# Another step order in a copy out of PSUM, pooled queries by two additions, and a new instruction order

## The chip, the core and the metric

The kernel runs on one core of one Trainium2 chip. TensorE (PE) multiplies matrices into PSUM, VectorE (DVE) and ScalarE (ACT) work element by element and read PSUM, GpSimd (POOL) works in SBUF and issues DMAs, SyncE (SP) issues DMAs only. The metric is the device time of the whole program in microseconds, given as the median of several runs.

## What is computed

Two layers follow each other. The first is an "hourglass" attention over 8 batches of 8 heads, 576 positions of 64 values each; the second sends each of the 4608 resulting rows to one of 8 experts. Cut to what matters:

```python
q_d = q.reshape(B, H, Sd, 4, D).mean(axis=3)      # the same for k_d, v_d
out_d = sm_attn(q_d, k_d, v_d)                    # softmax attention over 144 means
out_up = np.repeat(out_d, 4, axis=2)
mask = np.abs(pos[:, None] - pos[None, :]) < 4    # a band of 7 positions
out_local = softmax(where(mask, scale * q @ k.T, -1e9)) @ v
x = (out_up + out_local) as rows of 512
logits = x @ w_gate; e_idx = argmax(logits)       # one expert for each row
out[row] = gate_w * sigmoid(x @ w_output_gate)[e] * (relu(x @ w1[e]) @ w2[e])
```

## The kernel before, in words

The attention is done in 32 units, one for each pair of heads of a batch (`u = 4 b + hp`). After the four units of a batch comes its `gate` part, which routes the rows and stores them in DRAM. The experts run last, in tiles of 128 rows: `unit` gathers rows, transposes them, multiplies by w1 (L1074), takes the relu (L1016 on ACT, L1018 on DVE), multiplies by w2 (L1090), scales (L1099) and scatters (L1021).

A unit of attention begins with `prep(u)`. PE transposes q and then k of two heads (L641) from `blk` into a PSUM tile, which holds 576 f16 columns on 128 partitions. In PSUM the column of position 8 n + c is 72 c + n: positions that follow each other lie 72 columns apart. For q, DVE copies the tile as it is into `qT` (L651), and the reduce of L656 sums four positions each into `qd`, reading in steps of 72 columns. For k, ACT copies the tile into `kT` in the order of the positions (L665): it reads PSUM column after column, and writes SBUF in steps of 8 elements, 16 bytes. Then DVE sums four neighbours of `kT` into `kd` (L670) and scales them (L672).

`scores(u)` needs all of these. PE multiplies `kd` with `qd` (L690) and pools v (L695), ACT copies the pooled v (`vd`, L701), PE writes the other scores (L709, L717, L725), and ACT takes their exponential (`e`, L730). `values(u)` has the four groups of f32 matmuls L749, L755, L761 and L773. ACT forms the reciprocal of the sums as a logarithm and an exponential (`r`, L780 and L782), DVE multiplies (`u` L786, `xl` L794), POOL adds both parts into `xT` (L799), and ACT casts the result (L803). Two buffers hold `qT`, `qd`, `kT`, `kd`, `e` and `r`. Five PSUM tiles (S0, S1 of one bank, P0 to P2 of two) serve every user in turn.

Each engine carries out its instructions in the order in which they were written. That order comes from `Plan`: each task has an engine, an assumed duration, dependences and a priority; the plan takes, over and over, the task that can start first by its assumed times. `ADJ` adds a number to the priority of each kind of task. The assumed duration of L665 is 0.65 us before and after the change.

Of the kernel before, what the change touches and what calls it, by code (L numbers as in the profile page):

```python
# [8 lines left out]
F32 = mybir.dt.float32  # L9
F16 = mybir.dt.float16  # L10
I32 = mybir.dt.int32
ALU = mybir.AluOpType
AX = mybir.AxisListType
# [7 lines left out]
HB = 72  # L21
# [23 lines left out]


ADJ = {
# [6 lines left out]
    "mek": -365.54, "mek0": -101.99, "meq": 70.66, "meq0": 312.43, "out": -166.06, "prepk": -56.67,  # L54
# [5 lines left out]
}  # L60


# [3 lines left out]
def _ap(t, ap_list, extra_off=0):  # L66
    return bass.AP(tensor=t.tensor, offset=t.offset + extra_off, ap=ap_list)
# [263 lines left out]
def kernel(  # L331
# [11 lines left out]
    nc = tc.nc  # L343
    B, H, S, D = q.shape
# [15 lines left out]
    sb = ctx.enter_context(tc.tile_pool(name="sb", bufs=2))  # L360
# [12 lines left out]
    def v_qk(t):  # L373
        return t[0:HB].rearrange("p (h c) -> p h c", h=HP)
# [34 lines left out]
    plan = Plan()  # L409
    qb, vb = {}, {}  # L410

    def prio(u, kind, more=0.0):
        return 10.0 * u + OFF[kind] + more
# [79 lines left out]
    C = {}  # L493
# [121 lines left out]
        C["late"] = ts  # L615


    st = {}
    xb = {}

    def t16(T):
        return T.tile.bitcast(F16)[:, 0:S]

    def own(u):
        return "0" if u < 3 else ""

    def prep(u):
        b, hp = u // NP, u % NP
        d = st[u] = {}
        half = hp // 2  # L630
        h0 = 2 * (hp % 2)
        loads = [t for h in (2 * hp, 2 * hp + 1) for t in qb[b, half, "t"][h]]
        for i, nm in enumerate("qk"):
            T = Buf(r_T)
            src = qb[b, half][i]

            def fn(T=T, src=src):
                o = t16(T)
                for c in range(8):
                    for h in range(2):  # L640
                        nc.tensor.transpose(o[64 * h:64 * h + 64, HB * c:HB * c + HB],  # L641
                                            v_qk(src.tile)[:, h0 + h, D * c:D * c + D], id16[0:HB, 0:HB])
            hold = [Buf(r_qT), Buf(r_qd)] if i == 0 else [Buf(r_kT), Buf(r_kd)]
            tp = plan.add("PE", 0.29, fn, deps=[loads[0 + i], loads[2 + i], C["id"]], uses=[T, src] + hold,
                          prio=prio(u, "prep", i * 0.5), mode=12864, lat=0.1, name="prep" + nm + own(u), slow=0.5,
                          stream=(0.24, 0.45), ins=32)
            mean = hold[1]
            if i == 0:
                qT = d["qT"] = hold[0]
                d["qd"] = mean  # L650
                ev = plan.add("DVE", 0.46, lambda T=T, qT=qT: nc.vector.tensor_copy(qT.tile, t16(T)),  # L651
                              deps=[tp], uses=[T, qT], prio=prio(u, "ev"), name="qT" + own(u))

                def fn(mean=mean, qT=qT):
                    s = qT.tile[:, 0:1]
                    nc.vector.tensor_reduce(mean.tile.rearrange("p (n j i) -> p n j i", j=2, i=6),  # L656
                                            _ap(s, [s.ap[0], [6, 12], [4 * HB, 2], [1, 6], [HB, 4]]), axis=AX.X, op=ALU.add)
                e2 = plan.add("DVE", 0.75, fn, deps=[ev], uses=[qT, mean], prio=prio(u, "e2"), name="meq" + own(u))
            else:
                kT = d["kT"] = hold[0]  # L660
                d["kd"] = mean

                def fn(T=T, kT=kT):
                    s = t16(T)[:, 0:1]
                    nc.scalar.copy(kT.tile[:, 4:4 + S].rearrange("p (n c) -> p c n", c=8),  # L665
                                   _ap(s, [s.ap[0], [HB, 8], [1, HB]]))
                ev = plan.add("ACT", 0.65, fn, deps=[tp, C["z"]], uses=[T, kT], prio=prio(u, "ev", 0.5), name="kT" + own(u))

                def fn(mean=mean, kT=kT):
                    nc.vector.tensor_reduce(mean.tile.rearrange("p (g n) -> p g n", n=32)[:, :, 0:SW // 2],  # L670
                                            kT.tile[:, 4:4 + S].rearrange("p (g n m) -> p g n m", g=NGB, m=4), axis=AX.X, op=ALU.add)
                    nc.vector.tensor_scalar(mean.tile, mean.tile, scalar1=1.0 / 16, scalar2=None, op0=ALU.mult)  # L672
                e2 = plan.add("DVE", 0.93, fn, deps=[ev, C["z"]], uses=[kT, mean], prio=prio(u, "e2", 0.5), name="mek" + own(u))
            d[f"ev{i}"], d[f"e2{i}"] = ev, e2

    def scores(u):
# [427 lines left out]
    with tc.manual_schedule():  # L1104
# [8 lines left out]
        for u in range(NU):  # L1113
            prep(u)
# [16 lines left out]
        n = 0  # L1131
# [33 lines left out]
    with tc.If(v_most > 0):  # L1165
# [9 lines left out]
        for e in range(E):  # L1175
# [6 lines left out]
            with tc.For_i(0, n_more, 1):  # L1182
# [3 lines left out]
                for j in range(NJ * B):  # L1186
# [6 lines left out]
                    out=xg[:, 0, :], out_offset=None, in_=xs_dram.ap(),  # L1193
                    in_offset=bass.IndirectOffsetOnAxis(ap=fari, axis=0), bounds_check=N, oob_is_err=False)
                xgT, hs, yt = r_xgT.make(), r_hs.make(), r_y.make()
                t16 = singles[0].bitcast(F16).rearrange("p (j c n) -> p j c n", j=2, n=128)
                x16 = xg.bitcast(F16)
# [47 lines left out]
```

## Time and profile before

| what | us |
|---|---|
| median of 3 runs | 431.67 (428.96 to 432.05) |
| the profiled execution | 428.92 |
| its span, first to last instruction | 427.2 |
| ACT busy in it | 250.5 |
| PE busy in it | 357.7 |

The profiled execution lies 2.75 us below the median of the three. Its span leaves 1.72 us of its time outside. Busy time is the time in which an engine had an instruction under way; the PE clock column of the profile gives TensorE's granted clock as a share of full speed.

### The profile page before, as it was taken

How to read it: one execution, taken by the hardware profiler on the slowest of the kernel's cores; microseconds unless marked ns; L12 is line 12 of the kernel's file. 1: busy time of each engine (PE TensorE's matmuls, PEld its weight loads, DVE VectorE, ACT ScalarE, POOL GpSimd, SP SyncE). 2: the span in 40 equal slices, each digit the busy share in tenths (PEclk: the TensorE clock that was granted, in tenths of full speed). 3: DMA queues.
4: the chain of work that ended last, by engine and by line, in shares of the span. 5: the costliest groups of instructions: out<-in, count | busy, mean ns of one | idle time of the engine just before them, and what ended most of it. 6: DMA issues, size and time to landing. Idle time of an engine off the chain costs nothing.

```text
span 427.2 us, 15516 instructions
## 1 busy us (share of the span) xinstructions
PE 357.7 (84%) x6780; PEld 262.0 (61%) x6780; DVE 217.6 (51%) x494; ACT 250.5 (59%) x303; POOL 246.7 (58%) x328
## 2 busy tenths in 40 slices
PE   8776896878688679678888889999999999999930
PEld 3465675666466567466566577777667767767610
DVE  3655667577477488567596583822313322223210
ACT  5879868886676968886878754233243233343310
POOL 8446644454552536565243667777777888877120
PEclk9798798898798996999898899999999999999985
DMA  7967987969947985978875349986567776757120
GB/s 115 177 98 123 153 142 141 138 116 186 146 91 124 165 178 77 156 136 145 148 141 111 96 89 175 195 205 162 127 125 174 153 180 116 177 127 169 63 72 2
DMA packets 87665, 57.86 MB, mean 135 GB/s; under 512 B 53792, under 2 KB 84001, under 8 KB 87588
## 3 DMA queue, kind: packets, MB, share of 16 engines
q0 software_dynamic: 36864, 40.97, 55.2%
q1 hardware_dynamic: 50724, 15.81, 16.0%
q8 instruction: 55, 0.90, 0.9%
q14 instruction: 22, 0.18, 0.1%
HBM read 68.75 MB, written 15.24 MB: 197 GB/s over the span
## 4 chain that ended last, share of the span: by engine, by line
PE 57%; ACT 22%; DVE 12%; issue 4%; POOL 1%; POOLq 0%; DVEq 0%; ACTq 0%
ACT kT L665 15%; PE P L1090 10%; PE P L1074 9%; PE S L1074 7%; PE S L1090 6%; ACT e L730 3%; PE P L773 3%; PE P L761 3%; PE P L749 3%; PE P L755 3%; PE S L1146 2%; DVE qd L656 2%; PE S L695 2%; DVE kd L670 2%; ACT r L780 2%
## 5 line engine op out<-in xcount | busy, mean ns | idle before, releaser
L799 POOL TENSOR_TENSOR xT<-xl,u 128x576 f32<-128x576 f32 x32 | 43.5, 1359 | 119.7 <-DVE xl L794 83.1
L1074 PEld LDWEIGHTS <-blk 128*128 128x128 f16 x768 | 64.9, 98 | 14.7 <-issue 0.4
L1008 POOL DMA_DIRECT2D blk<-in_moe_w_dram x128 | 71.8, 582 | 1.4 <-PE P L1074 1.4
L665 ACT COPY kT<-S 128x576 f16<-128x576 f16 x25 | 68.6, 2762 | 2.1 <-PE S L641 2.0
L1021 POOL DMA_INDIRECT out_dram<-y,xg x40 | 40.8, 1021 | 28.0 <-ACT y L1099 17.4
L1090 PE MATMUL P<-blk,hs 128*128 128x512 f16 x200 | 49.7, 379 | 0.8 <-DVE hs L1018 0.8
L1074 PE MATMUL P<-xgT,blk 128*128 128x256 f16 (+1 forms) x432 | 49.6, 257 | 0.0
L670 DVE TENSOR_REDUCE kd<-kT 128x144 f16<-128x576 f16 x32 | 24.1, 752 | 48.4 <-ACT kT L665 46.1
L1090 PEld LDWEIGHTS <-hs 128*128 128x128 f16 x320 | 30.6, 98 | 29.0 <-DVE hs L1018 1.0
L1018 DVE TENSOR_SCALAR hs<-P 128x512 f16<-128x512 f32 x25 | 17.3, 690 | 55.7 <-PE P L1074 55.7
L730 ACT ACTIVATE e<-P 128x1008 f32<-128x1008 f32 x32 | 34.3, 1073 | 11.1 <-PE P L725 11.1
L780 ACT ACTIVATE r<-P 128x720 f32<-128x720 f32 x32 | 25.0, 781 | 25.2 <-PE P L761 25.1
L1040 POOL DMA_INDIRECT xg<-hx_xs,idx x31 | 32.3, 1043 | 12.4 <-issue 7.1
L656 DVE TENSOR_REDUCE qd<-qT 128x144 f16<-128x576 f16 x32 | 36.9, 1160 | 0.4
L1074 PE MATMUL S<-xgT,blk 128*128 128x256 f16 (+1 forms) x336 | 36.7, 252 | 0.0
L1016 ACT ACTIVATE hs<-P 128x512 f16<-128x512 f32 x21 | 12.5, 597 | 41.0 <-PE P L1074 38.5
L773 PE MATMUL P<-e,v 64*64 64x48 f32 x1536 | 33.6, 233 | 3.2 <-issue 3.2
L761 PE MATMUL P<-e,on_l 64*64 64x288 f32 x256 | 35.6, 503 | 0.0
L773 PEld LDWEIGHTS P<-e,v 64*64 64x64 f32 x1536 | 29.9, 146 | 7.1 <-issue 5.7
L641 PEld LDWEIGHTS <-blk 72*64 72x64 f16 x1024 | 22.9, 120 | 17.7 <-issue 15.7
L1090 PE MATMUL S<-blk,hs 128*128 128x512 f16 x120 | 30.2, 379 | 0.2 <-ACT hs L1016 0.2
L641 PE MATMUL S<-id,blk 72*64 72x72 f16 x768 | 22.0, 208 | 8.9 <-ACT kT L665 4.5
(159 smaller groups left out, 678.2 us busy)
## 6 DMA issues: line engine op xcount, KB each, us to landing
blk<-in_moe_w_dram POOLq DMA_DIRECT2D x128, 128.0 KB, 4.8
v<-in_v_dram SPq DMA_DIRECT2D x126, 84.0 KB
hx_xs<-xh SPq DMA_DIRECT2D x8, 580.5 KB
blk<-in_q_dram POOLq DMA_DIRECT2D x32, 144.0 KB, 4.9
blk<-in_k_dram POOLq DMA_DIRECT2D x32, 144.0 KB, 5.4
out_dram<-y,xg POOLq DMA_INDIRECT x40, 3.4
xg<-hx_xs,idx POOLq DMA_INDIRECT x31, 3.0
xg<-hx_xs,idx_e POOLq DMA_INDIRECT x9, 2.8
```

What stands on the lines that cost most here:

```text
L641: nc.tensor.transpose(o[64 * h:64 * h + 64, HB * c:HB * c + HB], v_qk(src.tile)[:, h0 + h, D * c:D * c + D], id16[0:HB, 0:HB])
L656: nc.vector.tensor_reduce(mean.tile.rearrange("p (n j i) -> p n j i", j=2, i=6), _ap(s, [s.ap[0], [6, 12], [4 * HB, 2], [1, 6], [HB, 4]]), ...
L665: nc.scalar.copy(kT.tile[:, 4:4 + S].rearrange("p (n c) -> p c n", c=8), _ap(s, [s.ap[0], [HB, 8], [1, HB]]))
L730: d["exp"] = plan.add("ACT", 1.01, lambda: nc.scalar.activation(e.tile, Sb.tile[:, :, 0:EC], AF.Exp, scale=scale), deps=[ls], uses=[Sb, e] ...
L761: nc.tensor.matmul(Nb.tile[64 * h:64 * h + 64, x, c:c + LC], lhsT=on_l[t], rhs=et[t, h, 0:LC], start=True, stop=True, skip_group_check=True)
L773: nc.tensor.matmul(Ob.tile[64 * h:64 * h + 64, x, c:c + SW], lhsT=vbuf.tile[t, NGB * h + g, :], rhs=et[t, h, SW * g:SW * g + SW], start=Tr ...
L780: nc.scalar.activation(r_.tile, _ap(s, [s.ap[0], [1, SD + S]]), AF.Ln)
L799: nc.gpsimd.tensor_tensor(xT.tile[:, hp, :].rearrange("p (g m c) -> p g m c", m=4, c=6), xl.tile.rearrange("p (g m c) -> p g m c", m=4, c= ...
L1008: nc.gpsimd.dma_start(v_w(bufs[i].tile, i)[:, c, f], src[:, c, f])
L1021: ins = nc.gpsimd.indirect_dma_start(out=out, out_offset=bass.IndirectOffsetOnAxis(ap=idx, axis=0), in_=yt, in_offset=None, bounds_check=N ...
L1074: nc.tensor.matmul(o, lhsT=v_w(wb[c // 2].tile, 0)[:, c % 2, 128 * f:128 * f + 128], rhs=xgT.tile[:, c, 0:nt], start=(c == 0), stop=(c == ...
L1090: nc.tensor.matmul(py.tile, lhsT=hs.tile[:, f, 128 * j:128 * j + 128], rhs=v_w(wb[2 + f // 4].tile, 2)[:, f % 4, :], start=(f == 0), stop= ...
```

## The change

Three things change. The copy of k (L665, after it L667) names the same elements in the other order: it reads PSUM in steps of 72 columns (144 bytes) and writes `kT` element after element. The pooled q is no longer one reduce of four elements each but two additions: the first adds the two halves of the four position classes into a new f32 tile `half_q` of 288 columns, the second adds two halves of that into `qd`. The table `ADJ` has new numbers and two assumed durations change (0.75 to 0.68 and 0.93 to 1.0), so that the instructions of every engine stand in another order.

```diff
-    "ca": 10.67, "cd": 178.57, "cm": -34.43, "co": 201.27, "cp": -21.63, "cw": -83.91, "down": -206.74,
+    "ca": 0.32, "cd": 135.05, "cm": 49.92, "co": 276.37, "cp": 26.08, "cw": -98.83, "down": -332.67,
...
+    half_q = sb.tile([128, 2, 2 * HB], F32, tag="half_q", name="half_q", bufs=1)
...
                 def fn(mean=mean, qT=qT):
-                    s = qT.tile[:, 0:1]
-                    nc.vector.tensor_reduce(mean.tile.rearrange("p (n j i) -> p n j i", j=2, i=6),
-                                            _ap(s, [s.ap[0], [6, 12], [4 * HB, 2], [1, 6], [HB, 4]]), axis=AX.X, op=ALU.add)
-                e2 = plan.add("DVE", 0.75, fn, deps=[ev], uses=[qT, mean], prio=prio(u, "e2"), name="meq" + own(u))
+                    s = qT.tile.rearrange("p (j m c) -> p j m c", j=2, m=2)
+                    nc.vector.tensor_tensor(half_q, s[:, :, 0, :], s[:, :, 1, :], op=ALU.add)
+                    s = half_q.rearrange("p j (m n i) -> p n j m i", m=2, i=6)
+                    nc.vector.tensor_tensor(mean.tile.rearrange("p (n j i) -> p n j i", j=2, i=6), s[:, :, :, 0, :], s[:, :, :, 1, :], op=ALU.add)
+                e2 = plan.add("DVE", 0.68, fn, deps=[ev], uses=[qT, mean], prio=prio(u, "e2"), name="meq" + own(u))
...
                     s = t16(T)[:, 0:1]
-                    nc.scalar.copy(kT.tile[:, 4:4 + S].rearrange("p (n c) -> p c n", c=8),
-                                   _ap(s, [s.ap[0], [HB, 8], [1, HB]]))
+                    nc.scalar.copy(kT.tile[:, 4:4 + S].rearrange("p (n c) -> p n c", c=8),
+                                   _ap(s, [s.ap[0], [1, HB], [HB, 8]]))
...
-                e2 = plan.add("DVE", 0.93, fn, deps=[ev, C["z"]], uses=[kT, mean], prio=prio(u, "e2", 0.5), name="mek" + own(u))
+                e2 = plan.add("DVE", 1.0, fn, deps=[ev, C["z"]], uses=[kT, mean], prio=prio(u, "e2", 0.5), name="mek" + own(u))
```

On ACT, around the ninth and tenth of the 32 copies of k (third batch), the kernel before has these rows; `vd` is the copy of pooled v, `e` the exponential, `r` the reciprocal's two steps, `x` the cast.

```order
L701 COPY vd<-S_88 128x192
L665 COPY kT_122<-S_87 128x8x72
L730 ACTIVATE e<-P_90 128x1008
L803 CAST x_1076<-xT 128x576
L665 COPY kT_120<-S_87 128x8x72
L780 ACTIVATE r<-P_91 128x720
L782 ACTIVATE r<-r 128x720
L701 COPY vd<-S_88 128x192
```

Each copy of k stands alone there, the tenth of the 32 between a `vd` and the `e` of another unit. The changed kernel has this for the ninth and tenth:

```order
L703 COPY vd<-S_87 128x192
L732 ACTIVATE e<-P_90 128x1008
L805 CAST x_1102<-xT 128x576
L732 ACTIVATE e<-P_89 128x1008
L667 COPY kT_120<-S_87 128x576
L667 COPY kT_122<-S_88 128x576
L782 ACTIVATE r<-P_91 128x720
L784 ACTIVATE r<-r 128x720
L782 ACTIVATE r<-P_91 128x720
```

The copies of two units now stand side by side, behind both exponentials and ahead of the `r` of both units.

On DVE at the same place the kernel before takes the means of the two units with other work between them:

```order
L656 TENSOR_REDUCE qd<-qT 128x144
L670 TENSOR_REDUCE kd_121<-kT_120 128x6x24
L672 TENSOR_SCALAR kd_121<-kd_121 128x192
L656 TENSOR_REDUCE qd<-qT 128x144
L786 TENSOR_TENSOR u<-P_90,r 128x6x2x12
L794 TENSOR_TENSOR xl<-P_90,r 128x576
L651 COPY qT<-S_88 128x576
```

In the changed kernel the two `kd` follow each other, and each `qd` is two instructions:

```order
L672 TENSOR_REDUCE kd_121<-kT_120 128x6x24
L674 TENSOR_SCALAR kd_121<-kd_121 128x192
L672 TENSOR_REDUCE kd_123<-kT_122 128x6x24
L674 TENSOR_SCALAR kd_123<-kd_123 128x192
L652 COPY qT<-P_89 128x576
L788 TENSOR_TENSOR u<-P_90,r 128x6x2x12
L652 COPY qT<-S_87 128x576
L985 COPY xh<-S_88 96x2x512
L657 TENSOR_TENSOR half_q<-qT 128x288
L659 TENSOR_TENSOR qd<-half_q 128x144
```

What moved is the grouping: the copies, the sums and the scores of two units stand in pairs, where before they alternated.

## Rows read from the trace of the kernel before

**Rows 1.** Windows by stage: busy us of each engine, PE clock, DMA share, GB/s.
```profile
0.00:14.00 14.00, 11.12 (x95) 4.68 (x95) 6.98 (x23) 9.52 (x9) 12.72 (x31) 1.00 0.86 136
14.00:262.00 248.00, 198.56 (x5430) 153.49 (x5431) 164.04 (x383) 189.08 (x212) 125.40 (x166) 0.89 0.78 134
262.00:411.00 149.00, 147.98 (x1258) 103.81 (x1255) 46.03 (x87) 51.42 (x83) 107.62 (x132) 1.00 0.68 151
411.00:427.20 16.20, 0.00 (x0) 0.00 (x0) 0.50 (x3) 0.53 (x1) 0.98 (x1) 0.55 0.06 17
```
**Rows 2.** The page's chain of work that ended last, shares of the span.
```profile
PE 57%; ACT 22%; DVE 12%; issue 4%; POOL 1%; POOLq 0%; DVEq 0%; ACTq 0%
ACT kT L665 15%; PE P L1090 10%; PE P L1074 9%; PE S L1074 7%; PE S L1090 6%; ACT e L730 3%; PE P L773 3%; PE P L761 3%; PE P L749 3%; PE P L755 3%; PE S L1146 2%; DVE qd L656 2%; PE S L695 2%; DVE kd L670 2%; ACT r L780 2%
```
**Rows 3.** Groups of instructions: shapes, count | busy us, mean ns | idle before.
```profile
L665 ACT COPY kT<-S 128x576 f16<-128x576 f16 x25 | 68.6, 2762 | 2.1 <-PE S L641 2.0
L656 DVE TENSOR_REDUCE qd<-qT 128x144 f16<-128x576 f16 x32 | 36.9, 1160 | 0.4
L803 ACT CAST x<-xT 128x576 f16<-128x576 f32 x32 | 24.5, 764 | 4.6 <-POOL xT L799 4.5
L670 DVE TENSOR_REDUCE kd<-kT 128x144 f16<-128x576 f16 x32 | 24.1, 752 | 48.4 <-ACT kT L665 46.1 <-ACT g_ez L908 1.3 <-ACT eo L880 1.0
L794 DVE TENSOR_TENSOR xl<-P,r 128x576 f32<-128x576 f32 x32 | 23.9, 747 | 3.0 <-ACT r L782 2.6 <-PE P L773 0.4
L665 ACT COPY kT<-P 128x576 f16<-128x576 f16 x7 | 19.5, 2789 | 3.2 <-PE P L641 3.2
L1016 ACT ACTIVATE hs<-S 128x512 f16<-128x512 f32 x19 | 11.3, 597 | 29.8 <-PE S L1074 29.8
L701 ACT COPY vd<-S 128x192 f32<-128x192 f32 x31 | 10.1, 327 | 7.2 <-PE S L695 7.2
L786 DVE TENSOR_TENSOR u<-P,r 128x144 f32<-128x144 f32 x32 | 9.7, 303 | 10.6 <-ACT r L782 8.8 <-PE P L773 1.6
L948 DVE TENSOR_TENSOR g_rr<-g_rr,rel 96x240 f16<-96x240 f16 x8 | 5.2, 656 | 0.3
```
**Rows 4.** Timeline of PE, ACT and DVE: start us, us, what, idle before and releaser.
```profile
69.26 2.73 ACT L665 COPY kT<-S 128x576 f16<-128x576 f16 x1 [1.08 <-PE S L641]
...
71.48 1.34 ACT L730 ACTIVATE e<-P 128x1008 f32<-128x1008 f32 x1
...
72.01 0.75 DVE L670 TENSOR_REDUCE kd<-kT 128x144 f16<-128x576 f16 x1 [1.97 <-ACT kT L665]
72.03 0.69 PE L641 MATMUL S<-id,blk 72*64 72x72 f16 x16 [1.82 <-ACT kT L665]
```
**Rows 5.** Sums over 14 windows with ACT at 3.95 us or more of 4, then nine under 2.
```profile
sum 56.00, PE 38.53 PEld 29.88 DVE 27.90 ACT 55.87 POOL 35.63; mean PE 2.75 PEld 2.13 DVE 1.99 ACT 3.99 POOL 2.54
sum 36.00, PE 31.99 PEld 23.75 DVE 30.58 ACT 13.74 POOL 10.55; mean PE 3.55 PEld 2.64 DVE 3.40 ACT 1.53 POOL 1.17
```
**Rows 6.** One fall of the clock; sum of ten windows like the second; timeline.
```profile
110.00:114.00 4.00, 1.14 (x32) 0.88 (x31) 1.80 (x4) 4.00 (x4) 2.71 (x5) 0.76 1.07 146
114.00:118.00 4.00, 3.98 (x34) 2.46 (x38) 3.04 (x6) 0.72 (x2) 0.00 (x0) 0.50 0.74 119
sum 40.00, PE 38.42 PEld 28.51 DVE 27.25 ACT 31.58 POOL 18.60; mean PE 3.84 PEld 2.85 DVE 2.72 ACT 3.16 POOL 1.86
61.74 0.47 PE L749 MATMUL P<-e,vd 128*64 128x144 f32 x4
62.92 0.65 PE L761 MATMUL P<-e,on_l 64*64 64x288 f32 x6
72.96 0.78 PE L749 MATMUL P<-e,vd 128*64 128x144 f32 x4
75.16 1.17 PE L761 MATMUL P<-e,on_l 64*64 64x288 f32 x6
```
**Rows 7.** A window with more transfers, columns as in rows 1.
```profile
260.00:280.00 20.00, 20.00 (x220) 15.10 (x219) 12.49 (x34) 7.09 (x14) 15.25 (x24) 1.00 1.10 205
```

More of the change, by code (lines that the diff above doesn't have):

```diff
@@ L47 @@
 ADJ = {
[6 rows of a table removed]
-    "mek": -365.54, "mek0": -101.99, "meq": 70.66, "meq0": 312.43, "out": -166.06, "prepk": -56.67,
[5 rows of a table removed]
[6 rows of a table added]
+    "mek": -498.53, "mek0": -67.51, "meq": 4.32, "meq0": 271.12, "out": -223.37, "prepk": -99.41,
[5 rows of a table added]
 }
```

20 rows, old and new, of the table ADJ are left out of this document.

## The prediction

> **What bounds the kernel now.** I read the windows by stage first [rows 1]. They cut the span of 427.2 us into four. The first 14 us fill the first buffers. From 14 to 262 us the 32 units of attention run. From 262 to 411 us PE is busy 147.98 of 149 us at a granted clock of 1.00: the experts are bound by PE. The last 16.2 us hold almost no work. The change touches only attention, so the other three stages, 14 + 149 + 16.2 us, stay as they are, and the question is how far the 248 us between them shrink.
>
> In those 248 us no engine is full: PE is busy 198.56 us (80%), ACT 189.08 (76%), DVE 164.04 (66%), POOL 125.40 (51%), and the DMA engines have a mean share of 0.78. So I went on to the chain of work that ended last [rows 2]. Its largest single line is ACT's copy of k, L665, with 15% of the span, and nearly everything else on it is PE. The groups [rows 3] say why: the 32 copies take 68.6 + 19.5 = 88.1 us, 2.75 us each. ACT moves 512 columns in 0.597 us elsewhere (L1016) and 576 in 0.764 us (L803). DVE stood idle for 46.1 us because the reduce behind the copy, L670, waited for it.
>
> The timeline shows one such place [rows 4]. The copy at 69.26 us runs for 2.73 us. PE's next transposes, L641, want the PSUM tile that the copy is still reading, and PE idles 1.82 us. DVE idles 1.97 us, and the exponential `e` that stands behind the copy on ACT begins only when the copy is at its end. One slow instruction thus stops three engines.
>
> A comparison of windows shows what PE does without that [rows 5]. I cut 14 to 262 us into 4 us pieces. In the 14 pieces where ACT is busy for 3.95 us or more, PE is busy 38.53 of 56 us, 69%. In the nine where ACT is busy under 2 us, PE reaches 31.99 of 36, 89%. PE is what runs when ACT lets it.
>
> The idle time has a second price [rows 6]. From 110 to 114 us PE was busy for 1.14 us only, and in the next 4 us its clock is at 0.50, the lower level of 1.2 GHz. Ten such windows sum to 40 us with PE busy for 38.42. At that clock four matmuls of L749 take 0.78 us instead of 0.47, and six of L761 1.17 instead of 0.65.
>
> **The copy of k.** The same 576 columns are copied, now with a stepping read from PSUM and a write in order. The trace has no such read on ACT, so I bound it. From below: ACT's in-order rows of 192 and 512 columns take 0.327 and 0.597 us [rows 3], 0.84 ns a column, so 576 columns cost 0.65 us; nothing in the edit makes it cheaper than an in-order copy, which excludes less. From above: 2.75 us, as now, if the step is as dear in the read as in the write (dearer still is a rival below). In between lies the one row with the same step of 72 f16 columns, DVE's L656. It reads 576 columns in 1.160 us where L670 reads as many neighbours in 0.752, so the step costs 0.41 us. That would make the copy 0.65 + 0.41 = 1.06 us. L656 is the nearest row by its step, but it reads SBUF; I take the middle of 0.65 and 1.06, 0.85 us.
>
> The rows show that the stepping write costs 2.1 us over an in-order copy [rows 3]. The Trainium skill (SBUF — State Buffer, Door 1: The DMA port swizzle) says that an access which goes to another 16-byte line each time pays a penalty, and that 16-bit elements lie eight to a line; a step of eight is just such a write, and the trace agrees that it is dear. But the skill also gives PSUM lines of 8 bytes there, and its page PSUM — Partial Sum Buffer (Specifications (TRN2)) says that patterns which are not contiguous slow matmuls down. If that held for ACT's read, each of the 576 elements, 144 bytes apart, would pay in its turn, which speaks against the change; no run here shows it. By that rule at the same price the copy would stay at 2.75 us and the sum below would lose its first term.
>
> On the chain the copy has 14.7% of 427.2 us, 62.8 us (the page rounds it to 15%) [rows 2]. Going from 2.75 to 0.85 us takes away 69% of that, **43 us**; with 0.65 it is 48, with 1.06 it is 39.
>
> **The pooled q.** One DVE reduce of 1.160 us goes, two additions come: 288 columns from f16 into f32 and 144 from f32 into f16. DVE's additions of 144 and 576 columns take 0.303 and 0.747 us [rows 3] (L786, L794), 1.03 ns a column, so 288 columns cost 0.45 and the pair 0.75 us. The dearest addition by the column, L948, has 240 in 0.656 us; at its 2.73 ns the pair would take 1.18 us, no gain. At the bare 1.03 ns a column, with no start, it would take 0.44. I take 0.75, from the rows of like shape: 0.41 us less, 13 us of DVE's 164 over 32 units. On the chain L656 has 2% (1.8% unrounded, 7.7 us) [rows 2], so **3 us** of it count. The additions follow each other on one engine, so the single `half_q` buffer makes nobody wait.
>
> **The new order.** It removes no work. The order on ACT now has two copies side by side, behind two exponentials and ahead of both `r`. At 0.85 us the `r` of two units waits 1.7 us behind them, no longer than behind the one copy of 2.75 us before; at 2.75 us each it would wait 5.5. On DVE the two `kd` then find their copies done. I cost the new order at nothing. What hides it is that ACT falls to 189 - 31 x 1.90 = 130 us of work; if the copies stay slow that cover is gone, which is part of the rivals. The assumed durations in the plan cost nothing on the chip by themselves.
>
> **The sum.** 43 + 3 = 46 us by the chain, if nothing ends later in its place. PE is what could, so I work it out from PE as well. The clock of 0.89 over the stage means 22% of 248 us, 55 us, at the lower level, and by the ten windows PE is busy for 96% of that, 52 us. L749 and L761 need 0.60 and 0.56 of the time at the full clock; at 0.57 PE's 198.56 us become 198.56 - 0.43 x 52 = 176 us. If PE then reaches the 89% of the pieces where ACT is free [rows 5], attention takes 198 us, 50 less; at 85% it takes 207, 41 less. Both ways meet at 46. ACT (130), DVE (151) and POOL (125) are then all below 202 us.
>
> The profiled execution took 428.92 us, 427.2 of span and 1.72 around it; minus 46 it is 383. The median of the runs lies 2.75 us higher, so I predict **386 us**. For this case the bounds of the copy (39 to 48) and of PE's share (41 to 50), with some falls of the clock left, give 376 to 396.
>
> **Rival 1: transfers set the pace.** In attention the DMA share is 0.78 over 248 us [rows 1], 193 us of transfers at a share of 1. In 202 us that is 0.96. For it: q, k, v and the experts' weights all come in this stage. Against it: the stretch from 260 to 280 us sustains 1.10 [rows 7]. If no more than 0.9 is reached, attention takes 215 us, 33 less: 399 us.
>
> **Rival 2: the change does not do what it says.** The stepping read costs what the stepping write did, and the copy stays at 2.75 us. Then only the 3 us of pooled q are left, and the pairs of copies put `r` later by up to 2.75 us at places where ACT is the one waited for: 425 to 437, near 430. For it speaks that the step alone makes L656 dearer than L670; against it that this is 0.41 us, a fifth of the 2.1 us that the write costs. The rule on PSUM lines of the Trainium skill (PSUM — Partial Sum Buffer, Specifications (TRN2)), carried over to ACT, would give this case.
>
> **Rival 3: slower.** The stepping read on ACT is dearer than the stepping write was. It decides from 2.75 us per copy. At twice the extra, 0.65 + 4.2 = 4.85 us, ACT's work rises by 31 x 2.1 = 65 us to 254; ACT would be full and alone the bound, with pairs of 9.7 us in front of both `r`. At 95% busy attention takes 267 us, 19 more: 451 us. No row speaks for it; the lack of any stepping read of PSUM on ACT is all that leaves it open.
>
> **How the numbers follow.** 0.60 for the forecast (376 to 396), 0.24 for transfers near 399, 0.08 for rival 2, 0.04 for rival 3, and 0.04 for attention faster than 376 allows. To hold eight in ten the range takes the forecast and most of rival 1, with the bounds of the copy inside it: 371 to 410. A measurement of this kernel can tell about 1% from no change. The forecast, rival 1 and the faster end are all faster by more: 0.88. Rival 2 is mostly within 1%, 0.06, and otherwise slower; with rival 3 that makes 0.06 slower.
>
> **What would show it.** The group of the copy at 0.65 to 1.06 us; the two additions near 0.45 and 0.30 us; L665's successor gone from the head of the chain; DVE's wait for it well under 46 us; PE at 85% or more between the first unit and the experts, with fewer windows at a clock of 0.50; the experts' stage again near 149 us, only earlier. A copy above 2 us makes the prediction wrong at its first term. A cheap copy with PE still near 80% would say that another wait took its place, and the DMA share of the stage says whether it is rival 1.

## The result and the profile after

The changed kernel takes 405.44 us (median of four runs, 404.26 to 407.25) where the kernel before, run beside it, takes 430.84 us (428.96 to 432.05): a ratio of 0.942, interval 0.937 to 0.947. Timed twice more, it gave 0.929 (0.920 to 0.939) and 0.945 (0.934 to 0.955). Some executions of a kernel are over 1.5% longer than its fastest; the ratios leave these out, the medians keep them, and the profiles of `e2_old_copy` and `e3_old_q` are of such executions. The gain is 25 us; the forecast was 46.

The profiled execution has a span of 405.5 us. Its windows by stage, with the columns of [rows 1]:

```profile
0.00:14.00 14.00, 12.19 (x123) 5.38 (x124) 6.96 (x27) 7.15 (x10) 11.07 (x27) 1.00 0.85 130
14.00:238.00 224.00, 191.44 (x5369) 145.51 (x5367) 152.28 (x404) 128.69 (x208) 123.19 (x164) 0.90 0.85 146
238.00:390.00 152.00, 150.63 (x1293) 105.95 (x1290) 48.60 (x94) 52.67 (x86) 111.09 (x138) 1.00 0.72 152
390.00:405.50 15.50, 0.00 (x0) 0.00 (x0) 0.28 (x2) 0.52 (x1) 0.98 (x1) 0.53 0.07 18
```

Attention takes 224 us instead of 248, and the other three stages are as they were. ACT fell from 189 to 129 us there and DVE from 164 to 152, as worked out. But PE, which was to fall from 199 to 176 us, stands at 191, and its clock at 0.90 instead of 0.89 [rows 1]: PE still spends much of the stage at the lower level.

The groups that answer to [rows 3]:

```profile
L672 DVE TENSOR_REDUCE kd<-kT 128x144 f16<-128x576 f16 x32 | 24.0, 749 | 22.7 <-ACT kT L667 22.6
L667 ACT COPY kT<-S 128x576 f16<-128x576 f16 x26 | 16.3, 637 | 10.5 <-PE S L642 10.3
L657 DVE TENSOR_TENSOR half_q<-qT 128x288 f32<-128x288 f16 x32 | 14.4, 451 | 0.5
L659 DVE TENSOR_TENSOR qd<-half_q 128x144 f16<-128x144 f32 x32 | 9.9, 308 | 1.1
```

The page's chain of work that ended last:

```profile
PE 66%; issue 11%; DVE 6%; POOL 5%; DMA 4%; ACT 3%; SPq 1%; POOLq 0%; DVEq 0%
PE P L1076 8%; PE P L1092 8%; PE S L1076 6%; PE S L1092 5%; PE P L751 5%; PE P L763 5%; PE P L775 4%; PE S L840 4%; PE P L757 4%; PE S L642 3%; PE S L981 3%; DMA v<-in_v_dram 2%; POOL out_dram L1023 2%; PE S L697 2%; PE P L642 2%
```

The copy takes 0.637 us instead of 2.762 and has gone from the chain, where it held 15% [rows 2]. What has come up there is "issue", from 4% to 11%: time in which an engine waited for nothing that the profile shows. PE's waits in attention say whose time that is (engine, tile and line, what it waited for: us in total, times, longest):

```profile
PE S L642 <- issue: 7.7, 4, 4.9
PE P L642 <- issue: 5.0, 4, 2.2
PE S L642 <- DVE xh L985: 3.3, 2, 2.2
PE P L727 <- issue: 3.2, 2, 2.1
PE P L775 <- issue: 2.9, 3, 1.9
PE S L697 <- issue: 2.2, 1, 2.2
PE S L697 <- DMA v<-in_v_dram: 2.2, 3, 1.6
```

No wait for the copy of k is among the seven. Five of the seven are "issue", and one of those waits lasts 4.9 us. The timeline around it (start us, us, what, idle before and releaser):

```profile
41.17 0.45 PE L642 MATMUL S<-id,blk 72*64 72x72 f16 x16
46.53 0.69 PE L642 MATMUL S<-id,blk 72*64 72x72 f16 x16 [4.91 <-issue]
...
47.26 0.64 ACT L667 COPY kT<-S 128x576 f16<-128x576 f16 x1 [3.87 <-PE S L642]
...
47.93 0.75 DVE L672 TENSOR_REDUCE kd<-kT 128x144 f16<-128x576 f16 x1 [3.97 <-ACT kT L667]
```

The windows over the same stretch:

```profile
42.00:46.00 4.00, 0.00 (x0) 0.00 (x0) 1.85 (x5) 1.38 (x2) 4.00 (x7) 1.00 1.21 218
46.00:50.00 4.00, 3.47 (x54) 2.10 (x55) 0.96 (x2) 1.65 (x3) 1.77 (x4) 0.57 1.20 189
```

The DMA queues from 43.5 to 45.5 us (packets, MB, share of the time of 16 engines):

```profile
q0 software_dynamic: 273, 0.26, 79.3%
q1 hardware_dynamic: 701, 0.17, 41.5%
q8 instruction: 1, 0.02, 3.4%
```

PE is idle from 41.62 to 46.53 us, and ACT and DVE wait for it: the chain of waits runs the other way round than in [rows 4]. While PE does nothing, the data queues are full (a share of 1.21) and one packet of a queue named "instruction", q8, goes through. Behind the wait the mean clock of the next 4 us is 0.57. The page's row of this queue for the whole execution:

```profile
q8 instruction: 55, 0.90, 0.9%
```

From the packed trace: that packet has 16,384 bytes and was under way from 43.89 to 44.98 us. The kernel moves 55 of them, 0.90 MB; PE carries out 6779 loads of weights and 6779 matmuls, so this is 66 bytes for each of these instructions, some 250 to the packet. That agrees with the 64 bytes of an instruction that the Trainium skill states (Perfetto Trace Analysis, The 4-stage abstract model); an estimate from that figure is 256 to the packet. The reading that the experiments test is then: **PE waits for its own program**, which comes in pieces of 256 instructions by DMA while attention's data fill the DMA engines. To measure it I counted all of PE's instructions that the trace has, in order of time: its loads and matmuls and the few semaphore instructions between them. I noted at which number, modulo 256 (what is left after division by 256), each of its waits over 0.1 us stands. Eight waits over 1 us stand at numbers 191 to 195 of 256 (a band of five in 256), and the longest of them is this one; all waits in the band sum to 22.3 us in attention, all others to 9.7 us. Before, it was 12.3 in the band, 2.6 of them a single wait for `kd` that happens to fall there, and 38.5 outside.

The landings of the packets say the same. Of PE's 19 waits over 0.5 us in attention 13 stand in the band, and each of these 13 ends between 1.36 and 1.63 us after a packet of q8 has landed; none of the other six does.

### The profile page after: what moved, and what is told of

It is laid out like the page before. It is cut to its first block, busy times and chain, and to the rows that moved or that the text cites. A ratio compares the mean times of both kernels' runs of the same rounds, so it can differ in the third digit from the quotient of the medians.

```text
span 405.5 us, 15537 instructions
## 1 busy us (share of the span) xinstructions
PE 354.3 (87%) x6779; PEld 256.8 (63%) x6779; DVE 208.1 (51%) x526; ACT 189.0 (47%) x303; POOL 246.3 (61%) x328
## 4 chain that ended last, share of the span: by engine, by line
PE 66%; issue 11%; DVE 6%; POOL 5%; DMA 4%; ACT 3%; SPq 1%; POOLq 0%; DVEq 0%
PE P L1076 8%; PE P L1092 8%; PE S L1076 6%; PE S L1092 5%; PE P L751 5%; PE P L763 5%; PE P L775 4%; PE S L840 4%; PE P L757 4%; PE S L642 3%; PE S L981 3%; DMA v<-in_v_dram 2%; POOL out_dram L1023 2%; PE S L697 2%; PE P L642 2%
## 5 line engine op out<-in xcount | busy, mean ns | idle before, releaser
L1092 PE MATMUL P<-blk,hs 128*128 128x512 f16 x192 | 48.6, 379 | 0.8 <-DVE hs L1020 0.8
L672 DVE TENSOR_REDUCE kd<-kT 128x144 f16<-128x576 f16 x32 | 24.0, 749 | 22.7 <-ACT kT L667 22.6
L732 ACT ACTIVATE e<-P 128x1008 f32<-128x1008 f32 x32 | 32.3, 1012 | 5.9 <-PE P L727 5.6
L775 PE MATMUL P<-e,v 64*64 64x48 f32 x1536 | 30.7, 223 | 2.9 <-issue 2.9
L1092 PE MATMUL S<-blk,hs 128*128 128x512 f16 x128 | 32.7, 379 | 0.0
L763 PE MATMUL P<-e,on_l 64*64 64x288 f32 x256 | 31.0, 447 | 0.0
L775 PEld LDWEIGHTS P<-e,v 64*64 64x64 f32 x1536 | 26.8, 136 | 5.2 <-issue 3.4
L642 PE MATMUL S<-id,blk 72*64 72x72 f16 x640 | 19.8, 213 | 11.8 <-issue 7.7
L1018 ACT ACTIVATE hs<-S 128x512 f16<-128x512 f32 x20 | 11.9, 597 | 35.9 <-PE S L1076 33.3
L1101 ACT ACTIVATE y<-P,xg 128x512 f32<-128x512 f32 x24 | 16.5, 687 | 23.2 <-PE P L1092 20.1
L784 ACT ACTIVATE r<-r 128x720 f32<-128x720 f32 x32 | 25.7, 805 | 0.9
```

What stands on the lines that cost most here:

```text
L732: d["exp"] = plan.add("ACT", 1.01, lambda: nc.scalar.activation(e.tile, Sb.tile[:, :, 0:EC], AF.Exp, scale=scale), deps=[ls], uses=[Sb, e] ...
L763: nc.tensor.matmul(Nb.tile[64 * h:64 * h + 64, x, c:c + LC], lhsT=on_l[t], rhs=et[t, h, 0:LC], start=True, stop=True, skip_group_check=True)
L775: nc.tensor.matmul(Ob.tile[64 * h:64 * h + 64, x, c:c + SW], lhsT=vbuf.tile[t, NGB * h + g, :], rhs=et[t, h, SW * g:SW * g + SW], start=Tr ...
L784: lx = plan.add("ACT", 0.8, lambda: nc.scalar.activation(r_.tile, r_.tile, AF.Exp, scale=-1.0), deps=[l1], uses=[r_], prio=prio(u, "rex"), ...
L1092: nc.tensor.matmul(py.tile, lhsT=hs.tile[:, f, 128 * j:128 * j + 128], rhs=v_w(wb[2 + f // 4].tile, 2)[:, f % 4, :], start=(f == 0), stop= ...
```

## The experiments

### One part of the change at a time

`e1_copy_only` is the kernel before with the new copy alone:

```diff
-                    nc.scalar.copy(kT.tile[:, 4:4 + S].rearrange("p (n c) -> p c n", c=8),
-                                   _ap(s, [s.ap[0], [HB, 8], [1, HB]]))
+                    nc.scalar.copy(kT.tile[:, 4:4 + S].rearrange("p (n c) -> p n c", c=8),
+                                   _ap(s, [s.ap[0], [1, HB], [HB, 8]]))
```

> The kernel before with the copy of k alone in its new step order; table, order and pooled q as before. If the copy is the cause of the gain and the old order can use it, the copy takes 0.64 us as in the changed kernel and the time falls by some 20 of the 25 us, to about 410. If the gain needs the new order (the rival), the copy is as short but the time stays above 420.

Measured: 407.29 us, ratio 0.950 (0.941 to 0.959). Its group of the copy, and DVE's reduce behind it:

```profile
L670 DVE TENSOR_REDUCE kd<-kT 128x144 f16<-128x576 f16 x32 | 23.8, 745 | 6.5 <-ACT kT L665 6.2
L665 ACT COPY kT<-S 128x576 f16<-128x576 f16 x25 | 15.9, 640 | 1.1 <-PE S L641 0.9
```

Two lines of the diff bring a gain whose interval overlaps that of the whole change.

`e2_old_copy` is the changed kernel with the old copy:

```diff
-                    nc.scalar.copy(kT.tile[:, 4:4 + S].rearrange("p (n c) -> p n c", c=8),
-                                   _ap(s, [s.ap[0], [1, HB], [HB, 8]]))
+                    nc.scalar.copy(kT.tile[:, 4:4 + S].rearrange("p (n c) -> p c n", c=8),
+                                   _ap(s, [s.ap[0], [HB, 8], [1, HB]]))
```

> The changed kernel with the copy of k in its old step order (2.75 us); new order and new pooled q kept. If the new order is worth something by itself, the time stays below 428. If it only suits a short copy, two copies of 2.75 us side by side make every reciprocal late and the time is 435 to 450, slower than before.

Measured: 436.79 us, ratio 1.0095 (1.0047 to 1.0144): the new order and the additions, without the fast copy, cost 1%. Its group of the copy, and DVE's reduce behind it:

```profile
L667 ACT COPY kT<-S 128x576 f16<-128x576 f16 x26 | 70.9, 2783 | 0.6 <-PE S L642 0.5
L672 DVE TENSOR_REDUCE kd<-kT 128x144 f16<-128x576 f16 x32 | 24.1, 753 | 67.0 <-ACT kT L667 67.0
```

The lines of its chain:

```profile
ACT kT L667 14%; PE P L1092 5%; PE P L1076 4%; PE S L1076 4%; PE P L751 3%; ACT e L732 3%; PE P L763 3%; POOL out_dram L1023 3%; PE P L775 3%; PE P L757 3%; POOL blk L1010 3%; POOL xT L801 3%; PE S L1092 2%; ACT x L805 2%; POOL xg L1042 2%
```

The copy is back at 2.78 us and at the head of the chain with 14%. So the new order does need the cheap copy. That its pairs of copies are the reason, as the prediction had it, is not shown: in the trace two copies follow each other directly on ACT at five of 31 places, against three in the kernel before. What grew is DVE's wait for the copy, 67.0 us against 46.1 [rows 3]; how the 1% comes of it stays open.

`e3_old_q` is the changed kernel with the one reduce for the pooled q:

```diff
-                    nc.vector.tensor_tensor(half_q, s[:, :, 0, :], s[:, :, 1, :], op=ALU.add)
...
+                    nc.vector.tensor_reduce(mean.tile.rearrange("p (n j i) -> p n j i", j=2, i=6),
+                                            _ap(s, [s.ap[0], [6, 12], [4 * HB, 2], [1, 6], [HB, 4]]), axis=AX.X, op=ALU.add)
```

> The changed kernel with the one reduce for pooled q, 1.16 us instead of 0.45 + 0.31. DVE gets 13 us more work. If DVE is off the path, as its 6% of the chain of the changed kernel says, the time rises by 0 to 3 us, to 405 to 408. If DVE has become a second bound it rises by 6 us or more.

Measured: 403.13 us, ratio 0.937 (0.930 to 0.944), no slower than the whole change. Its windows show the 13 us of DVE's work that the additions save (165 against 152 us); attention is about 1 us longer for it:

```profile
14.00:239.00 225.00, 189.05 (x5365) 144.34 (x5365) 165.09 (x375) 128.45 (x208) 123.75 (x166) 0.92 0.84 146
```

### PE and its program

`f1_shift` cuts 84 pieces of the matmuls with which PE fills its time in the first microseconds into smaller ones, so that 126 more instructions of PE stand ahead of attention and nothing else changes:

```diff
+        split = [84]
...
-                m = min(n, w)
+                m = min(n, w if split[0] <= 0 else 1)
+                split[0] -= 1
```

> The changed kernel with 126 more instructions on PE at its start: the first fillers are cut into pieces of 128 columns, so that the columns are the same and every later instruction stands 126 places further in PE's program. Theory: PE stalls where its next 256 instructions have not come yet. Then the long stalls of attention that the profile puts down to nothing come again at places 193 or 194 past a multiple of 256, thus 126 instructions earlier in the work, at other lines; the time is within 1.5% of 405. Rival: the stalls are waits for q, k or v, so they stay at the same lines (the 4.9 us stall at the transposes near 42 us, for one) and only their count of instructions moves by 126.

Measured: 402.17 us, ratio 0.934 (0.925 to 0.942). In its trace the long waits stand in the same band of numbers again, 21.4 us in all, so at other places of the program, 126 instructions earlier. In this trace 15 waits over 0.5 us stand in the band, and each ends between 1.25 and 1.60 us after an instruction packet has landed. The longest but one, in the timeline of PE:

```profile
138.65 0.20 PE L727 MATMUL P<-qT,kT 64*56 64x48 f16 x3
141.49 0.44 PE L727 MATMUL P<-qT,kT 64*56 64x48 f16 x21 [2.65 <-issue]
```

PE stops for 2.65 us inside one run of 24 matmuls that all read the same `qT` and `kT`, after the third. No operand can be what it waited for. An instruction packet was under way from 138.83 to 140.00 us. That the waits go by a count of instructions, wherever in the program that count falls, is what a wait for data can't do.

`f3_twice_v` was to make the DMA engines fuller: each load of v is issued twice.

```diff
+                    if 0 < u < NU - 1:
+                        nc.sync.dma_start(t[:, n0:n1, :], _ap(s, [[D, KR], [2 * SW * D, n1 - n0], [1, D]], o + 2 * SW * D * n0))
```

> The changed kernel with each load of v issued twice, the second with the same data to the same place (all but the first and last unit's): some 40 us more of transfers in attention, nothing more to compute. Theory: pieces of PE's program come late because they share the DMA engines with data. Then the stalls at 193 or 194 past a multiple of 256 grow well over the 22 us of the changed kernel, to 35 us or more, and the time rises by 15 us or more. Rival: the pieces come late for a reason of their own; the stalls stay near 22 us, and any loss stands at waits for v.

Measured: 635.2 us, ratio 1.455 (1.445 to 1.465). It doesn't tell the theories apart. PE's largest wait in its attention:

```profile
PE S L699 <- DMA v<-in_v_dram: 167.9, 28, 11.4
```

The engines of its chain:

```profile
DMA 44%; PE 40%; issue 5%; SPq 3%; POOL 3%; DVE 2%; ACT 1%; POOLq 0%; DVEq 0%; ACTq 0%
```

The second load of a piece goes into the buffer of the first and waits for it: SyncE stands 309.8 us, 120 times, for a load of v to land. PE waits 167.9 us for v with the DMA engines at a share of 0.51. The load on the queues went down and not up; the waits in the band were 13.7 us. The experiment was built wrongly for its purpose.

`f4_no_qk4` leaves out the loads of q and k from the fifth batch on; the units there work on what lies in the buffers.

```diff
+                    key = (bufs[i].banks, h0)
+                    if b >= 4 and key in filled:
...
+                        return
+                    filled.add(key)
```

> The changed kernel without nearly all loads of q and k for batches 4 to 7: PE transposes there what the buffers hold, so the attention weights of these batches are not the reference's; all instructions but 30 DMAs stand. Theory: with fewer transfers the pieces of PE's program come in time, and the stalls of the second half of attention (11 of the 22 us) fall below 4 us, some falls of the clock go with them, and the time falls by 8 to 20 us. Rival: the stalls do not depend on transfers; the time falls by less than 4 us.

Measured: 397.27 us, ratio 0.906 (0.902 to 0.910), 2.5% better than the changed kernel in its runs on the same chip (0.929, 0.920 to 0.939). The second halves of attention, in the changed kernel from 135 us and here from 130 us:

```profile
135.00:238.00 103.00, 90.09 (x2505) 68.95 (x2498) 72.38 (x198) 58.87 (x97) 54.31 (x67) 0.90 0.80 143
```

```profile
130.00:230.00 100.00, 87.83 (x2473) 67.82 (x2469) 71.31 (x195) 58.31 (x96) 43.58 (x52) 0.91 0.63 120
```

The DMA share falls from 0.80 to 0.63. The waits in the band fall from 10.3 us (changed kernel) and 10.1 us (the same in `r1_after`) to 6.3 us. That is the direction that the theory wants, but not the fall below 4 us that I expected, and POOL has 11 us less to do in that half as well. So this run alone does not settle whether full DMA engines are what makes the packets late.

`f5_few` and `g2_wide_val` change how many instructions PE needs. The last matmuls of `values(u)`, six of 48 columns, become one of 288, with one v group for all six; in `f5_few` it is always the first group.

```diff
-            for g in range(NGB):
...
-                        c = DL * (1 - x) + SW * g
-                        nc.tensor.matmul(Ob.tile[64 * h:64 * h + 64, x, c:c + SW], lhsT=vbuf.tile[t, NGB * h + g, :],
-                                         rhs=et[t, h, SW * g:SW * g + SW], start=True, stop=True, skip_group_check=True)
+                    c = DL * (1 - x)
+                    nc.tensor.matmul(Ob.tile[64 * h:64 * h + 64, x, c:c + LC], lhsT=vbuf.tile[t, NGB * h + ONE[b][hp], :],
+                                     rhs=et[t, h, 0:LC], start=True, stop=True, skip_group_check=True)
```

> The changed kernel with the last matmuls of a unit (weights times v) as 4 of 288 columns in place of 24 of 48, so that each uses the wrong v for most columns: 80 of some 337 PE instructions of a unit fewer for the same columns, about ten pieces of 256 less over attention. The matmuls themselves get shorter by 0.2 to 0.3 us a unit, 6 to 10 us. Theory: fewer pieces are asked for per us, so the stalls at the ends of pieces fall too, from 22 to 16 us or less, and the time by 12 to 25 us in all. Rival: stalls are not a matter of PE's instruction count; only the shorter matmuls count, 5 to 10 us.

Measured: 610.18 us, ratio 1.393 (1.388 to 1.399). That time says nothing of PE: with these values more than 640 rows went to one expert, and a path at the end that handles the rest took some 220 us. Attention itself, which lies ahead of that, took 206 us, with 6.0 us of waits in the band. For a time that can be read, `g2_wide_val` chooses the group for each unit (table `ONE`) so that no expert gets too many rows.

> The changed kernel with PE's last matmuls of values(u) (L775 of the changed kernel) written as one of 288 columns where there were six of 48; all six position groups are multiplied by one group's v, so the result differs from the reference; which group, is chosen for each unit so that no expert gets more than 640 rows and the experts' stage stays as it was. The columns that PE streams and the bytes moved are as before, PE's instructions in attention fall by 2560 of 10785, ten pieces of 256. Theory (PE waits for its own program, in pieces of 256): the waits at one index modulo 256 fall from 20 to 22 us in attention to 10 us or less, although the stage is shorter and so its DMA share higher; attention ends at 220 us or earlier instead of 237.6, the time comes to 385 to 392 us. Rival (transfers set the pace, or PE waits for data): those waits stay near 20 us, only the 7 us go that PE is busy less in these matmuls, the stage takes 216 us or more and the time is 398 us or more.

Measured: 386.58 us (385.44 to 389.46), ratio 0.905 (0.895 to 0.915). The window of its attention:

```profile
14.00:218.00 204.00, 177.01 (x4099) 126.03 (x4087) 153.57 (x405) 127.76 (x209) 122.82 (x164) 0.93 0.92 160
```

PE's largest waits in it:

```profile
PE S L643 <- DVE xh L985: 4.8, 4, 2.3
PE P L712 <- ACT vd L704: 4.6, 6, 2.9
PE S L698 <- DMA v<-in_v_dram: 4.1, 4, 2.1
```

The group of the changed line:

```profile
L775 PE MATMUL P<-e,v 64*64 64x288 f32 x256 | 23.1, 426 | 0.0
```

The page's row of the instruction queue:

```profile
q8 instruction: 45, 0.74, 0.8%
```

2560 instructions less are ten packets less, 45 instead of 55, which fixes the 256 to a packet. The waits in the band fall to 4.3 us. The "issue" rows have gone from the top of PE's waits; the largest has 1.7 us. The DMA engines carry the same bytes in less time, at a share of 0.92.

`h1_half_val` goes the other way: each of these matmuls of 48 columns becomes two of 24.

```diff
+                        for w in range(SW * g, SW * g + SW, SW // 2):
+                            c = DL * (1 - x) + w
+                            nc.tensor.matmul(Ob.tile[64 * h:64 * h + 64, x, c:c + SW // 2], lhsT=vbuf.tile[t, NGB * h + g, :],
+                                             rhs=et[t, h, w:w + SW // 2], start=True, stop=True, skip_group_check=True)
```

> The changed kernel with each matmul of 48 columns at L775 written as two of 24, the result unchanged. Columns and bytes as before, PE's instructions in attention rise by 3072 to 13857, twelve pieces more. Theory (PE waits for its own program): the waits at one index modulo 256 rise from 20 to 22 us to 27 us or more, with more falls of the clock behind them; on top of that PE is busy some 20 us more, since a matmul of 24 columns takes little less than one of 48; the time is 430 us or more. Rival (no such waits): only PE's busy time grows, the sum of these waits stays within 18 to 24 us, and the time is 410 to 425 us.

Measured: 440.97 us, ratio 1.036 (1.022 to 1.049), slower than the kernel before. The same four views, first the window of attention:

```profile
14.00:271.00 257.00, 217.81 (x6916) 173.98 (x6917) 150.42 (x405) 128.86 (x209) 123.75 (x163) 0.91 0.74 130
```

PE's largest waits in it:

```profile
PE P L776 <- issue: 12.8, 9, 3.7
PE P L727 <- issue: 6.1, 6, 1.6
PE S L697 <- issue: 4.4, 2, 3.9
```

The group of the changed line:

```profile
L776 PE MATMUL P<-e,v 64*64 64x24 f32 x3072 | 60.2, 220 | 13.0 <-issue 12.8
```

The row of the instruction queue:

```profile
q8 instruction: 67, 1.10, 1.0%
```

Twelve packets more, as many as 3072 instructions make, and the waits in the band rise to 32.8 us, although the DMA share is lower (0.74). Of the 38 us that this kernel takes longer than `r1_after`, 29 are busy time of PE in attention: a matmul of 24 columns takes 220 ns and one of 48 takes 223, so halving them doubles their sum. The waits in the band are 10 us longer than in `r1_after`.

The changed kernel itself, timed and profiled beside both:

> The changed kernel once more, beside the two others on the same chip. Both theories: 400 to 411 us, ratio to the kernel before 0.93 to 0.945; the waits at one index modulo 256 between 19 and 26 us in attention, as in its two profiled executions so far.

Measured: 402.96 us, ratio 0.945 (0.934 to 0.955). Another timing of it, beside `f3_twice_v`, `f4_no_qk4` and `f5_few` on one chip:

> The changed kernel once more, on the chip of the next three, as their measure: 402 to 408.

Measured: 411.02 us, ratio 0.929 (0.920 to 0.939).

Nine of the profiles in one table, worked out from the packed traces: attention from 14 us to its last matmul of `values`, PE's instructions of every kind in it, PE's waits over 0.1 us in and outside the band, PE's time at the lower clock level, and its busy time (us).

```
kernel          attention  PE instr.  in band  outside  lower clock  PE busy  DMA share
before              245.3      10877     12.3     38.5         54.6    196.0       0.77
after               223.6      10785     22.3      9.7         44.4    191.1       0.85
r1_after            219.3      10818     23.2      8.3         37.6    188.0       0.85
e1_copy_only        219.5      10867     20.2     14.8         23.9    184.3       0.87
f1_shift            217.8      10786     21.4      7.5         37.6    188.4       0.86
f4_no_qk4           215.7      10801     14.4     13.1         37.6    188.3       0.74
f5_few              206.0       8227      6.0     20.8         30.7    178.7       0.90
g2_wide_val         203.1       8187      4.3     22.1         27.3    176.1       0.92
h1_half_val         256.7      13890     32.8      7.1         47.8    217.5       0.74
```

What the reader is to see: the waits in the band go by the number of PE's instructions for each microsecond, from 4 to 6 us at 40 instructions to 33 us at 54. Only `f4_no_qk4` falls out, with 14 us at 50: it is the one with fewer transfers. Before, the slow copy held PE up and so gave the next piece of program time to arrive. The median piece of 256 took PE 5.9 us there, and its packet had landed 2.8 us (median) before PE went on with it. In the changed kernel a piece takes 4.7 us and its packet lands 1.6 us ahead, close to the 1.4 to 1.6 us with which the waits above end; so 22 us of waiting come of it. That it is the copy and not the new order, `e1_copy_only` shows with 20.2 us, and `e2_old_copy`, which is not in the table, with 7. With a quarter fewer instructions the waits nearly vanish, with more they grow.

The table also gives an idea of what they are worth. From `r1_after` to `g2_wide_val` the waits in the band fall by 19 us, but those outside rise by 14: the work behind them (`xh`, `vd`, v's loads) is not much earlier, and PE waits for that instead. Of the 16 us between the two kernels 8 are the matmuls themselves (31.1 us for the line in `r1_after`, against 23.1), 4.3 are idle time, and the rest is the clock (10 us less at the lower level, at 0.43 of the time). Two profiles of the changed kernel itself, `after` and `r1_after`, lie 4 us apart.

## Why the prediction was right, and where it was short

**The copy of k: right.** Predicted 0.85 us between 0.65 and 1.06; measured 0.637, just under the lower bound that the in-order rows gave. Against that estimate, reading PSUM in steps of 144 bytes costs ACT nothing that shows. Rival 2, and with it Rival 3, fall by this row. The rule on PSUM lines (the Trainium skill, PSUM — Partial Sum Buffer, Specifications (TRN2)) speaks of matmuls; carried over to ACT's reads it doesn't hold at this step. `e2_old_copy` shows the other side, 2.78 us for the same elements with the steps in the write, and `e1_copy_only` that this alone brings all of the gain that can be told from noise.

**The pooled q: right in its size, wrong in its worth.** The additions take 0.451 and 0.308 us (predicted 0.45 and 0.30) and DVE has 13 us less to do. But the 3 us that I put on the chain did not show: `e3_old_q` is as fast without the additions, though the intervals are too wide to exclude 3 us. The chain's share of L656 was read before the copy was gone. In the changed kernel DVE still waits 22.6 us for the copy of k, which speaks for room on DVE.

**The new order: costed at nothing, and worth nothing that can be measured.** `e1_copy_only` with the old order has 0.950 (0.941 to 0.959), the whole change 0.942 (0.937 to 0.947). Its cover was the cheap copy; without it, the order costs 1%.

**The sum: 46 us forecast, 25 measured.** The term that was mis-sized is the first, 43 us for the copy: `e1_copy_only`, which changes the copy alone, gains 5.0%, 21 us (18 to 25). I had put all of the copy's share of the chain down as gain, on the condition that nothing ends later in its place. The step that failed is the cross-check from PE, which was there to test this condition. It had two terms, PE's busy time and its busy share, and its forecast of 202 us is set against 224. That both ways met at 46 was no confirmation: both left out that another wait could follow the copy.

- PE's busy time was to be 176 us, on the assumption that all 55 us at the lower clock go. They fell to 44.4 us, in which PE is busy 41.7; at the 0.57 of [rows 6] these cost 0.43 x 41.7 = 18 us. Without them PE would stand at 173. This term is 15 us short.
- The busy share was to be 85 to 89%. It is 191.44 of 224, 85%, at the low end: 33 us of idle time instead of 26. This is the other 7 us.

Behind both stand in part the waits that no line of my argument had. [Rows 4] and [rows 6] showed falls of the clock behind waits for other engines, and I took the copy for their cause. In the changed kernel seven of the nine stretches at the lower clock begin within, or less than 3 us after, a wait of over 1 us for the program; in the kernel before it is two of ten. PE's own program took over as what stops it, and the clock fell as before. The page of the kernel before had shown a sign: "issue" with 4% of the chain [rows 2]. I read it as a remainder, and called nearly everything beside the copy PE, where PE has 57% and DVE 12%.

How much of the missing 21 us hangs on this is estimated and not settled. With the band nearly empty (`g2_wide_val`) attention takes 203.1 us, 16 less than `r1_after`, of which 8 are the fewer matmuls. So some 8 us of this pair of runs go with PE's program, idle time and clock taken together; they are worked out and not measured by themselves. The rest is in part clock that falls for other reasons as well (27.3 us are left there, some 10 us of PE time), which the forecast also took to be gone.

**Rival 1, transfers set the pace at a DMA share of 0.9 or less: refuted as it was put.** Its time (399 us) lay nearer to the result than mine, but `g2_wide_val` moves the same bytes through attention at a share of 0.92, in 204 us. The transfers of data aren't the limit; PE's instructions, which come over the same DMA engines, were late.

**The range was right with some luck.** 405 us lie inside 371 to 410, but outside the forecast's own 376 to 396. The range reached to 410 for the sake of rival 1, and what rival 1 had for a reason did not happen. The bounds that I named for the forecast, 39 to 48 us with the 3 us of q and 41 to 50 us, give only 381 to 391; how far beyond them it reaches was not worked out.

**What would show it.** Copy, additions, chain and the experts' stage (152 us, PE busy 150.63) came as listed; DVE's wait for the copy is 22.6 us instead of 46. PE at 85% was just met; the time at the lower clock fell only from 54.6 to 44.4 us. "Another wait took its place" is what happened, though not one that any line of the kernel names.

## What to carry to other kernels

When ACT rearranges a tile from PSUM to SBUF, put the steps into the PSUM read and write SBUF in order: here 0.64 against 2.76 us for 576 f16 elements on 128 partitions. Before pricing a gain on an engine with thousands of small instructions, read the "issue" share of the chain and look whether its waits stand at a fixed count of instructions. If they do, fewer and wider instructions may pay as well: here 2560 fewer took another 16 us, in a kernel that multiplies by one v group and so gives other results. And don't credit all the time at the lower clock to the wait that you remove: it goes only if no other wait takes its place.

## What the runs showed of the hardware

- PE's program arrives during the run, in packets of 16,384 bytes with 256 instructions (45, 55 and 67 packets for 2560 fewer, as many, and 3072 more instructions). With attention's data on the DMA engines, PE stood still for up to 4.9 us at a time at one number of 256, close to 193 as I count them, and went on after such a packet had landed: 44.98 us landed, 46.53 us resumed; 140.00 and 141.49 in `f1_shift`. In none of the nine profiles of the table did PE pass that number in attention less than 1.0 us after the landing of the packet that goes with it. What PE does in that time no run shows, and how much the data on the DMA engines delay a packet is not settled.
- A matmul of 24 columns costs what one of 48 costs (220 and 223 ns in f32, 64 rows), while one of 288 takes 426 ns: six of 48 take 1.34 us, one of 288 a third of that. In sum over the line it is 30.7 against 23.1 us of busy time only, since the small ones overlap.
- ACT's read of PSUM in steps of 144 bytes costs nothing that shows (0.637 us for 576 columns, against an estimate of 0.65 in order); its write to SBUF in steps of 16 bytes does (2.762 us).
